# Where the attention mask of batches 1 and 2 is applied: a multiply on VectorE in place of an accumulating matmul on TensorE

## The chip, the cores and the metric

The kernel runs on one core of one Trainium2 chip. The metric is the device time of one execution in microseconds (us); the kernel before takes 332.73 us, the median of three runs (332.69 to 332.88). Engines are named as in the profile: PE is the matrix engine (PEld is its weight load), DVE the vector engine, ACT the scalar engine with the exponential, POOL the engine that issues most of the loads, SP the one that issues the stores and the DMA transposes.

## The reference

Sparse attention over 8 batches, 8 heads, 576 positions and 64 values per head, followed by a feed-forward block on the 4608 tokens:

```python
scores = scale * np.matmul(q, k.transpose(0, 1, 3, 2))
rel = pos[:, None] - pos[None, :]
mask_local = (rel >= 0) & (rel < 32)                                    # heads 0 to 3
mask_strided = (rel >= 0) & (pos[None, :] % 32 == pos[:, None] % 32)    # heads 4 to 7
scores = np.where(masks[None], scores, -1000000000.0)
attn = softmax(scores)                                                  # over the last axis
x = (attn @ v)    # rearranged to [4608 tokens, 512]
h = x @ w_in                                                            # 512 -> 2048
r = np.maximum(h, 0.0)
out = (s * (r * r) + b) @ w_out                                         # 2048 -> 512
```

## The kernel before

Only the tiles of the score matrix that the mask lets through are computed. Heads are taken in pairs: a batch has two local pairs (m = 0, 1) of 6 tiles each, 128 keys by 2 x 96 queries, and two strided pairs (m = 2, 3) of 8 tiles each, 72 keys by 2 x 72 queries. A group of tiles (2 local or 3 strided) shares a PSUM bank and one exponential. The mask is applied in one of two ways, chosen by the batch number `b`. Line numbers of the profile that matter here: 426 is the mask matmul, 429 the score matmul, 443 the exponential, 451 the multiply by the mask.

```python
    TB, SB, AB, F1B, F2B = 1, 2, 1, 2, 2
    PE_MASK = 3
    ps = {tag: [psum.tile([128, PS], FP32, name=f"ps_{tag}{i}") for i in range(n)]
          for tag, n in (("t", TB), ("s", SB), ("a", AB), ("f1", F1B), ("f2", F2B))}
    # ...
        per_s = 2 if loc else 3

        def score(i, group):
            g, n = i // per_s, min(per_s, nt - i // per_s * per_s)

            def f():
                # ...
                if b < PE_MASK:
                    nc.tensor.matmul(                                    # L426
                        out=st["s", g][0:nk, c:c + 2 * nq], lhsT=ident[0:nk, 0:nk],
                        rhs=neg_loc if loc else neg_str, start=True, stop=False)
                nc.tensor.matmul(                                        # L429
                    out=st["s", g][0:nk, c:c + 2 * nq], lhsT=(...),      # k of the tile
                    rhs=st["q"][:, i].rearrange("d e c -> d (e c)"), start=b >= PE_MASK, stop=True)

            s = Step(f, (2 if b < PE_MASK else 1) * (2 * nq / 2.4 + 8), needs=[("q", id_), ("k", id_)],
                     group=group if i % per_s == 0 else None)
            # ...
                def ex(eng):
                    pt = ptp.tile([128, 2 * per_s, nq], FP16, tag="pt" + sfx,
                                  bufs=7 if loc else 6, name="pt")
                    nc.scalar.activation(                                # L443
                        out=pt[0:nk, 0:2 * n].rearrange("k t c -> k (t c)"),
                        in_=st["s", g][0:nk, 0:2 * n * nq], func=AF.Exp, scale=scale)

                def ms(eng):
                    mask = (mask_loc if loc else mask_str)[:, None, :].to_broadcast([nk, 2 * n, nq])
                    nc.vector.tensor_tensor(                             # L451
                        out=pt[0:nk, 0:2 * n], in0=pt[0:nk, 0:2 * n], in1=mask, op=ALU.mult)

                s.posts = [([key], {"A": 170 + 0.83 * 2 * n * nq}, ex, [("e", id_, g), group]),
                           ([("e", id_, g)], {"V": 150 + 0.52 * 2 * n * nq}, ms, [("p", id_, g)])]
                if b < PE_MASK:
                    s.posts = [([key], {"A": 170 + 0.83 * 2 * n * nq}, ex, [("p", id_, g), group])]
```

`neg_loc` and `neg_str` hold 0 where the mask lets through and -30000 elsewhere; the identity times that tile, accumulated under the scores, makes the exponential 0 there. `mask_loc` and `mask_str` hold 1 and 0. The tiles `pt` are then weights for the product with v (line 481); its column of ones gives the sum of each row, so that the division (reciprocal 496, multiply 507) needs no reduction. The normalized x is transposed (529, or by DMA for the local pairs from batch 2 on) into `xT`, of which the feed-forward block reads 512 tokens at a time (a block, `T`; 9 in all):

- 574: first projection, 64 matmuls of 512 columns for a block; ACT or DVE applies the relu (592, 594), DVE squares (598, into `gT`).
- 609: second projection, again 64 matmuls; DVE scales and adds the bias (620) and the result is stored. For block 0, 16 matmuls more (632) make the bias term.

The order of all this is fixed when the program is built. A planner keeps a clock (`plan.t`), in which a step on PE has the length given to `Step`, and every piece of follow-up work has a cost for each engine that may do it; it takes the engine that would end first, and the next PE step whose inputs are ready on this clock:

```python
    def step_ready(self, s):
        r = self.ready_at(s.needs)
        # ... and the PSUM group's bank must be released
    # ...
        if cand is not None and (att_done < due() or main is None):
            s = att[cand][at_i[cand]]        # a step of attention
            plan.emit(s)
        elif main == 1:
            plan.emit(f1[i1])                # first projection
        elif main == 2:
            plan.emit(f2[i2])                # second projection
        elif i1 >= 16 or not keep_running(plan.next_time()):
            plan.advance()                   # nothing is ready: the plan's clock moves on
```

Semaphores keep the data right whatever the real times are; the plan only decides the order in each engine's stream. Loads of q and k of batch b + 2 are issued once batch b's transposes are planned and v of batch b + 1 is fetched, and loads of v of batch b + 2 once batch b's products with v are planned.

Of the kernel before, what the change touches and what calls it, by code (L numbers as in the profile page):

```python
# [110 lines left out]
def kernel(  # L111
# [202 lines left out]


    TB, SB, AB, F1B, F2B = 1, 2, 1, 2, 2
    PE_MASK = 3
    ps = {tag: [psum.tile([128, PS], FP32, name=f"ps_{tag}{i}") for i in range(n)]
          for tag, n in (("t", TB), ("s", SB), ("a", AB), ("f1", F1B), ("f2", F2B))}

# [18 lines left out]
    def pair_steps(b, m):  # L339
# [76 lines left out]
        def score(i, group):  # L416
# [3 lines left out]
            def f():  # L420
                if i % per_s == 0:
                    st["s", g] = bank(group)
                c = i % per_s * 2 * nq
                if b < PE_MASK:

# [4 lines left out]
                    out=st["s", g][0:nk, c:c + 2 * nq], lhsT=(st["k"][:, i * nq:i * nq + nk] if loc else st["k"][:, i, 0:SQ]),  # L430
# [4 lines that stand above are left out]
            if i % per_s == n - 1:  # L435
# [11 lines left out]
                def ms(eng):  # L447
# [8 lines left out]
                            [("p", id_, g)])]  # L456
                if b < PE_MASK:
                    s.posts = [([key], {"A": 170 + 0.83 * 2 * n * nq}, ex, [("p", id_, g), group])]
# [445 lines left out]
```

The softmax here doesn't subtract the row's maximum and nothing guards it: scores larger than these inputs give would overflow.

## Time and profile before

| | before |
|---|---|
| time, median of 3 runs | 332.73 us |
| span of the profiled execution | 330.6 us |
| PE busy, matmuls | 322.2 us (97%), 2480 |
| DVE busy | 193.4 us (58%), 529 instructions |
| ACT busy | 170.4 us (52%), 321 |
| POOL busy | 85.6 us (26%), 123 |
| mask matmuls (line 426) | 36 of 192 columns, 48 of 144; first and last start 9.7 and 80.3 us |
| multiplies by the mask (line 451) | 60, 20.0 us in all; first and last start 87.6 and 198.2 us |

The page gives busy times per engine, the span in 40 slices of 8.3 us (each digit a tenth of busy time), the chain of work that ended last, and groups of instructions by line. A matmul's duration in it is its latency; matmuls overlap, and the step from one to the next is read from the view in order of time. Attention work ends at about 200 us on PE's stream and the rest of the span is feed-forward alone.

### The profile page before, as it was taken

What the parts mean: (1) busy time and instruction counts of PE and PEld (TensorE: products, weight loads), DVE (VectorE), ACT (ScalarE), POOL (GpSimd) and SP (SyncE); (2) the same over time, 40 slices, a digit from 0 to 9 for tenths busy, and PEclk for the clock granted to TensorE, in tenths of its full rate; (3) what the DMA queues carried; (4) which work ended last, traced back from release to release, by engine and by line L of the source; (5) the groups of instructions that cost most, each with busy time, mean ns of one, the idle gap of its engine ahead of it and who ended that gap; (6) DMA issues with size and microseconds to landing.
All of it is one profiled execution on the core that took longest, in us unless ns stands there. A gap on an engine that the chain in (4) does not pass through costs nothing.

```text
span 330.6 us, 6484 instructions
## 1 busy us (share of the span) xinstructions
PE 322.2 (97%) x2480; PEld 185.0 (56%) x2480; DVE 193.4 (58%) x529; ACT 170.4 (52%) x321; POOL 85.6 (26%) x123
## 2 busy tenths in 40 slices
PE   8998999999999999999999999999999999999995
PEld 3764755567666566566665665544544544444442
DVE  6657638587886877778778866633333333333311
ACT  3766833388788576587576753331432433243100
POOL 6481657810944624724710000000000000000000
PEclk9999999999999999999999999999999999999999
DMA  8999999996797996995995003010001100101021
GB/s 118 183 165 204 215 170 164 220 174 70 116 137 99 165 94 132 169 107 101 187 110 91 32 15 87 20 47 32 32 32 43 54 32 35 63 3 62 32 95 63
DMA packets 73176, 32.80 MB, mean 99 GB/s; under 512 B 54586, under 2 KB 67514, under 8 KB 73146
## 3 DMA queue, kind: packets, MB, share of 16 engines
q0 software_dynamic: 50032, 18.65, 57.8%
q1 hardware_dynamic: 23114, 13.74, 18.1%
q8 instruction: 19, 0.31, 0.4%
q14 instruction: 11, 0.09, 0.1%
HBM read 38.15 MB, written 9.44 MB: 144 GB/s over the span
## 4 chain that ended last, share of the span: by engine, by line
PE 87%; DMA 7%; POOL 2%; ACT 2%; issue 1%; DVE 0%; SPq 0%; POOLq 0%; ACTq 0%
PE ps_f L609 37%; PE ps_f L574 35%; DMA ql<-in_q_dram 5%; PE ps_s L429 4%; PE ps_a L481 4%; PE ps_t L357 3%; DMA w_out_sb<-in_v_dram 2%; PE ps_t L529 1%; PE ps_s L426 1%; PE ps_a L632 1%; ACT qD_loc L286 1%; POOL w_in L273 1%; POOL v_loc L286 1%; PE ps_f L481 0%; ACT kT_loc L286 0%
## 5 line engine op out<-in xcount | busy, mean ns | idle before, releaser
L609 PE MATMUL ps_f<-w_out_sb,gT 128*128 128x512 f16 x576 | 148.7, 379 | 0.0
L592 ACT ACTIVATE u<-ps_f 128x512 f16<-128x512 f32 x136 | 80.7, 597 | 87.5 <-PE ps_f L574 72.9
L574 PE MATMUL ps_f<-xT,w_in_sb 128*128 128x512 f16 x432 | 116.0, 379 | 0.8 <-DMA w_in_sb<-in_moe_w_in_dram 0.8
L598 DVE TENSOR_TENSOR gT<-u 128x512 f16<-128x512 f16 x144 | 59.4, 418 | 62.6 <-ACT u L592 62.0
L609 PEld LDWEIGHTS <-gT 128*128 128x128 f16 x576 | 54.2, 98 | 54.0
L574 PEld LDWEIGHTS <-w_in_sb 128*128 128x128 f16 x432 | 46.1, 113 | 34.8 <-DMA w_in_sb<-in_moe_w_in_dram 1.2
L443 ACT ACTIVATE pt<-ps_s 128x384 f16<-128x384 f32 (+2 forms) x96 | 43.7, 488 | 16.0 <-PE ps_s L429 14.8
L620 DVE SCALAR_TENSOR_TENSOR o<-ps_f,s_sb,bcs 128x512 f32<-128x512 f32 x36 | 26.8, 745 | 22.9 <-PE ps_f L609 22.9
L507 DVE TENSOR_TENSOR x_nat<-ps_a,rec 72x256 f16<-72x256 f32 (+1 forms) x76 | 34.9, 460 | 1.2
L481 PEld LDWEIGHTS <-pt 72*72 72x72 f16 (+1 forms) x448 | 29.3, 120 | 10.8
L574 PE MATMUL ps_f<-xT,w_in 128*128 128x512 f16 x136 | 35.2, 379 | 0.1
L260 POOL DMA_DIRECT2D v_loc<-in_v_dram x28 | 24.1, 871 | 2.0 <-DMA ql<-in_q_dram 0.7
L496 DVE RECIPROCAL rec<-ps_a 72x4 f32<-72x4 f32 (+1 forms) x76 | 13.7, 180 | 17.2 <-PE ps_a L481 16.4
L574 PEld LDWEIGHTS <-w_in 128*128 128x128 f16 x144 | 15.3, 114 | 11.0
L265 POOL DMA_DIRECT2D v_str<-in_v_dram x16 | 13.8, 865 | 16.2 <-PE ps_a L481 6.8
L429 PE MATMUL ps_s<-qD_str,kTs 128*72 128x144 f16 x128 | 16.3, 226 | 0.2 <-ACT kTs L286 0.2
L429 PE MATMUL ps_s<-qD_loc,kT_loc 128*128 128x192 f16 x96 | 16.1, 246 | 0.3 <-ACT kT_loc L286 0.2
L481 PE MATMUL ps_a<-v_str,pt 72*72 72x65 f16 x204 | 15.5, 197 | 0.0
L429 PEld LDWEIGHTS <-kTs 128*72 128x72 f16 x128 | 12.0, 114 | 4.0 <-ACT kTs L286 0.4
L286 ACT COPY qD_loc<-ps_t 64x576 f16<-64x576 f16 x16 | 10.1, 633 | 3.7 <-PE ps_t L357 3.6
L529 PEld LDWEIGHTS <-x_nat 72*128 72x128 f16 (+1 forms) x152 | 8.8, 98 | 5.4 <-DVE x_nat L507 1.2
L664 POOL COPY gate<-kTs 1x1 f16<-1x1 f16 x8 | 2.0, 251 | 37.6 <-DMA kTs<-ks 37.6
(92 smaller groups left out, 295.7 us busy)
## 6 DMA issues: line engine op xcount, KB each, us to landing
out_dram<-o SPq DMA_DIRECT2D x36, 256.0 KB, 2.0
ql<-in_q_dram POOLq DMA_DIRECT2D x8, 288.0 KB, 5.1
kl<-in_k_dram POOLq DMA_DIRECT2D x8, 288.0 KB, 6.3
v_loc<-in_v_dram POOLq DMA_DIRECT2D x28, 80.0 KB, 9.1
w_out_sb<-in_moe_w_out_dram POOLq DMA_DIRECT2D x4, 512.0 KB, 11.8
qs<-in_q_dram POOLq DMA_DIRECT2D x6, 288.0 KB, 8.0
ks<-in_k_dram POOLq DMA_DIRECT2D x6, 288.0 KB, 8.6
v_str<-in_v_dram POOLq DMA_DIRECT2D x16, 72.0 KB, 6.9
```

Of the source, the lines that this page charges most:

```text
L260: nc.gpsimd.dma_start(out=vl[:, h, 1:LT, 0:D], in_=rest[:, h])
L265: nc.gpsimd.dma_start(out=vs[:, h, :, 0:D], in_=v[b, 4 + h].rearrange("(p j) d -> p j d", j=ST))
L286: {"A": nc.scalar.copy, "V": nc.vector.tensor_copy, "P": nc.gpsimd.tensor_copy}[eng](**kw)
L429: nc.tensor.matmul(out=st["s", g][0:nk, c:c + 2 * nq], lhsT=(st["k"][:, i * nq:i * nq + nk] if loc else st["k"][:, i, 0:SQ]), rhs=st["q"][ ...
L443: nc.scalar.activation(out=pt[0:nk, 0:2 * n].rearrange("k t c -> k (t c)"), in_=st["s", g][0:nk, 0:2 * n * nq], func=AF.Exp, scale=scale)
L481: nc.tensor.matmul(out=st["a"][0:nq, j % per, :], lhsT=st["pt", g][0:nk, i, :], rhs=vt[0:nk, 2 * mm + e, j, :])
L507: nc.vector.tensor_tensor(out=st["x"][:, j0:j0 + per, 64 * e:64 * e + 64], in0=st["pa", e, j][0:nq, 0:per, 0:D], in1=st["rec", e, j][0:nq, ...
L574: nc.tensor.matmul(out=gts["h", T, ft], lhsT=(w_in_sb[min(ft // 4, 2) - 1][:, ct, :] if ft > 3 else w_in0[ct]).rearrange("p (c x l) -> p c ...
L592: nc.scalar.activation(out=gts["u", T, ft], in_=gts["h", T, ft], func=AF.Relu)
L598: nc.vector.tensor_tensor(out=gts[T][:, ft, :], in0=u, in1=u, op=ALU.mult)
L609: nc.tensor.matmul(out=gts["o", T, ts], lhsT=gts[T][:, ft, ts * 128:(ts + 1) * 128], rhs=w_out_sb[:, ft, :], start=(ft == 0), stop=(ft == ...
L620: nc.vector.scalar_tensor_tensor(out=o, in0=gts["o", T, ts], scalar=s_sb[:, 0:1], in1=bcs, op0=ALU.mult, op1=ALU.add)
```

## The change

The constant `PE_MASK` goes from 3 to 1. It is the number of batches whose mask is added by a matmul. With 3, batches 0, 1 and 2 use the matmul, and batches 3 to 7 the multiply on DVE; with 1, batch 0 alone uses the matmul. It is for taking matmuls from the engine with the most work and giving DVE the masking of batches 1 and 2.

The words that came with the change ("First quarter of w_in in four transfers; k transposed by DMA from batch 4 on and ahead of the next loads; work on later transfers placed later, in place of: First quarter of w_in in four transfers") tell of other things, which both kernels contain. The whole difference between the two programs' texts is this:

```diff
-    PE_MASK = 3
+    PE_MASK = 1
```

The constant is read in four places, all of them shown above: whether the mask matmul is issued, whether the score matmul starts the accumulation, the length of the step on the plan's clock, and whether a multiply on DVE is posted.

## The prediction

> **What bounds the kernel now.** I read the page from the top (busy shares, slices), then the chain of work that ended last, then the matrix engine's (PE's) waits, and last the stretch from 35 to 90 us as a table by stage and in order of time, because only there does batch 1 or 2 run.
>
> ```profile
> PE 322.2 (97%) x2480; PEld 185.0 (56%) x2480; DVE 193.4 (58%) x529; ACT 170.4 (52%) x321; POOL 85.6 (26%) x123
> PE   8998999999999999999999999999999999999995
> DVE  6657638587886877778778866633333333333311
> PE 87%; DMA 7%; POOL 2%; ACT 2%; issue 1%; DVE 0%; SPq 0%; POOLq 0%; ACTq 0%
> ```
>
> The reader is to see that PE is busy nearly everywhere and is 87% of the chain that sets the end; VectorE (DVE) never appears in that chain, though it is 60 to 90% busy up to slice 27. "Busy" alone would not prove a bound, since matmuls overlap. The waits do. Nine are listed for PE in the whole span, the longest 1.1 us at the very start; these are three of them, and none lies between 67 and 90 us:
>
> ```profile
> PE ps_f L574 <- DMA w_in_sb<-in_moe_w_in_dram: 0.8, 1, 0.8
> PE ps_t L529 <- ACT kT_loc L286: 0.3, 1, 0.3
> PE ps_s L429 <- ACT kT_loc L286: 0.2, 1, 0.2
> ```
>
> So after about 35 us, PE waits for almost nothing: its instruction stream is the clock. The table by stage shows what the other engines do meanwhile (columns: stretch, length, busy us and instructions of PE, PEld, DVE, ACT, POOL, then clock, DMA share, GB/s):
>
> ```profile
> 38.00:44.00 6.00, 6.00 (x65) 4.60 (x63) 2.40 (x5) 4.65 (x11) 1.94 (x3) 1.00 1.10 204
> 44.00:50.00 6.00, 6.00 (x29) 2.74 (x28) 1.14 (x3) 0.60 (x1) 4.05 (x5) 1.00 1.81 160
> 61.00:66.40 5.40, 4.99 (x57) 3.13 (x56) 2.42 (x8) 2.37 (x5) 3.99 (x5) 1.00 1.23 249
> 66.40:72.00 5.60, 5.60 (x62) 3.97 (x59) 5.16 (x15) 4.97 (x12) 1.58 (x2) 1.00 1.83 188
> ```
>
> DVE has ample room from 38 to 50 us (3.5 busy of 12) and is crowded from 66.4 to 72 (5.16 of 5.60). The cost of a mask matmul is not its 227 or 246 ns, which is latency, but the step from one start to the next:
>
> ```profile
> 38.30 0.24 PE L429 MATMUL ps_s<-qD_loc,kT_loc 128*128 128x192 f16 x1
> 38.38 0.24 PE L426 MATMUL ps_s<-neg_loc,ident 128*128 128x192 f16 x1
> 38.46 0.25 PE L429 MATMUL ps_s<-qD_loc,kT_loc 128*128 128x192 f16 x1
> 74.87 0.23 PE L426 MATMUL ps_s<-neg_str,ident 72*72 72x144 f16 x1
> 74.94 0.23 PE L429 MATMUL ps_s<-qD_str,kTs 128*72 128x144 f16 x1
> 75.00 0.23 PE L426 MATMUL ps_s<-neg_str,ident 72*72 72x144 f16 x1
> 123.18 0.54 PE L429 MATMUL ps_s<-qD_str,kTs 128*72 128x144 f16 x6
> ```
>
> Start to start is 80 to 85 ns for a local mask (I use 83) and 60 to 70 ns for a strided one (65). The last line is a later batch, without mask matmuls: six scores in 0.54 us, so (0.54 - 0.226) / 5 = 63 ns each. Scores don't become slower when their masks go; each mask removed gives its whole step back.
>
> **What the Trainium skill says.** "TensorE: Matmul & The Clock Gate", section "Back-to-back issue gap", gives N/2.4 + 2.5 ns for a warm isolated gap: 82.5 ns at 192 columns and 62.5 at 144. The trace agrees (83 and 65). The same section gives 131 ns sustained at 512 columns; this trace has 216 (1.08 us for five in the chain in order of time), and I use the trace's. "VectorE: DVE Perf Modes", section "The perf-mode tier table", puts a 16-bit `tensor_tensor` in SBUF at the doubled rate; the mask multiply at 384 elements takes 348 ns against 549 for the multiply of the same size that reads PSUM, which fits. "SBUF — State Buffer", section "Who interferes with whom", says that a DVE operation with two SBUF inputs contends with GpSimd instructions that read SBUF, and infers that descriptor generation isn't hit. The trace agrees as far as it goes: the 15 multiplies from 140 to 170 us, while POOL issues loads, take 4.90 us together, and the 15 from 170 to 200 us, with POOL idle, 4.94. So I charge nothing for contention.
>
> **The change part by part.** The words given with the change name transfers and a transpose by DMA; the diff alters one constant, and both kernels hold those things. What remains: batches 1 and 2 lose the matmul that adds the mask before the exponential and gain a DVE multiply after it, as batches 3 to 7 already have.
>
> *Removed from PE.* Per batch 2 local pairs of heads x 6 tiles and 2 strided pairs x 8. For two batches 24 local and 32 strided: 24 x 0.083 + 32 x 0.065 = 1.99 + 2.08 = 4.1 us, half in each batch.
>
> *Added to DVE.* One multiply per score group. Per batch 6 local groups of 384 elements, 4 strided of 432 and 2 of 288. For two batches 12 x 0.348 + 8 x 0.364 + 4 x 0.295 = 8.3 us (means from the groups by shape). DVE would go from 193.4 to about 201.7 us busy.
>
> *Moved.* The order of every engine's stream is fixed ahead by a planner inside the kernel, which simulates the run with its own costs. The shorter score steps and new posts shift its clock after batch 1's first score (35 us), so later interleaving is redrawn, and some copies go from DVE to ACT. Nothing before 35 us should move.
>
> *Batch 2 (65 to 81 us), on the path.* PE has the first projection of token block 1 to fill with, and DVE's delay only makes batch 2's results later. Those are first needed for block 2: block 1 still has 128 matmuls x 0.216 = 27.6 us from 66.5 us on, besides attention work. DVE takes 4.1 us more where 65 to 81 us holds 12.7 busy of 16, and ACT 12.8; that spills, but the whole stretch from 89 to 200 us runs with multiplies on DVE at 75 to 83% and PE busy in all but 0.14 us. So I count batch 2's saving in full: 2.0 us.
>
> *Batch 1 (35 to 43 us), only partly on the path.* Its multiplies are hidden: exponentials end by 44 us and the first product with v runs at 50.3 us, when v has arrived. But its PE time was filler too. From 44 to 64.7 us, PE fills with the second projection of block 0 (64 matmuls and 16 for the bias), and at its end it needs batch 1's last x transposed: the ACT copy to xT ends at 66.16, and block 1 starts at 66.46. If v's landing and the chain product, reciprocal, multiply, transpose, copy keep their times, 2 us saved at 40 us return as a hole before 66 us. Against that, DVE waits 1.5 us there for the product at 62.93, while PE works through second-projection matmuls that the planner put ahead; with less filler that chain tightens. I count 60%: 1.2 us.
>
> *Sum.* 2.0 + 1.2 = 3.2 us, less 0.5 us for the redrawn order (PE now idles little from 67 to 231 us, so redrawing can hardly improve it): 2.7 us saved, 332.7 - 2.7 = 330.0 us.
>
> **The rivals.** *Everything is returned (4.1 us).* For: PE is 87% of the chain. Against: the tight end of batch 1. It would give 328.6 us. *DVE becomes the bound in batch 2.* For: 5.16 of 5.60 us busy from 66.4 to 72. If 2 to 4 us of holes appear, the time is 331 to 333. Against: there is a block of filler, ACT can take copies, and the later batches run so. *The hole before block 1 takes all of batch 1's saving and the longer latency more:* 330.7 to 332. For: the 0.35 us wait at 65.06 shows that the edge is already reached. *An unlucky order* delays a fetch of a later batch (fetches wait for earlier steps of the plan) and opens a hole of several us: 334 to 338. Against: v and q/k are fetched about one block ahead; in the profile, PE waits for none of these loads after 35 us.
>
> **Range and chances.** The gain is limited by 4.1 us, 1.2% of the time, so "faster by over 2%" needs something the diff doesn't contain. Low end: full gain and a little luck in the order, 328.3. High end: batch 1's saving lost and 2 us of new holes, 332.9. Slower by over 2% needs about 7 us of holes, only by the last rival: 3%.
>
> **What would show each step.** Mask matmuls from 84 to 28 and none after about 17 us; DVE multiplies by a mask from 60 to 84; DVE busy near 201 us. Batch 2: no new PE wait on DVE from 67 to 100 us. Batch 1: the first projection of block 1 starts at 65 to 66 us, instead of 66.46, with about 1 us of PE idle from 50 to 66. From 231 us on, the same stream, 2 to 4 us earlier. I am wrong if PE waits for a masked tile or for `gT` for over 1 us in total, if a fetch of a later batch shows up among PE's waits, or if block 1 starts no earlier than before.

## The result, and the profile after

The changed kernel takes 329.91 us (median of six, 328.95 to 330.71), the kernel before 332.70 (six, 332.63 to 332.88): ratio 0.9912, 95% interval 0.9895 to 0.9929. Measured again on another chip, it took 329.53 us against 332.67, ratio 0.9893 (0.9873 to 0.9912). It is faster, by about 1%.

The page of the changed kernel, busy shares, slices and chain:

```profile
PE 318.7 (97%) x2424; PEld 181.7 (55%) x2424; DVE 201.2 (61%) x552; ACT 171.6 (52%) x322; POOL 84.8 (26%) x123
PE   8898899999999999999999999999999999999995
DVE  5566946698877768676878777586442423332311
PE 85%; DMA 7%; ACT 4%; POOL 2%; issue 1%; DVE 0%; SPq 0%; POOLq 0%
```

PE lost exactly the 56 mask matmuls. DVE gained 7.8 busy us and is still absent from the chain; ACT went from 2% of it to 4%. One thing shows that nobody asked for: DVE's busy stretch reaches two or three slices further to the right. Mask matmuls and multiplies, by line:

```profile
L426 PE MATMUL ps_s<-neg_str,ident x16: 223/226/233, 14.5 to 18.6; 72*72 72x144 f16 x16
L426 PE MATMUL ps_s<-neg_loc,ident x12: 242/246/249, 10.4 to 13.5; 128*128 128x192 f16 x12
L451 DVE TENSOR_TENSOR pt<-pt,mask_loc x42: 320/357/361, 38.5 to 212.5; 128x384 f16<-128x384 f16 x42
L451 DVE TENSOR_TENSOR pt<-pt,mask_str x42: 293/370/380, 41.6 to 224.5; 72x432 f16<-72x432 f16 x28, 72x288 f16<-72x288 f16 x14
```

The last multiply starts at 224.5 us, against 198.2 before. The same stretches as before, and PE's waits for other engines that matter:

```profile
38.00:44.00 6.00, 5.65 (x56) 3.82 (x55) 5.83 (x17) 5.36 (x13) 2.12 (x3) 1.00 1.07 210
44.00:50.00 6.00, 6.00 (x31) 2.75 (x29) 1.26 (x4) 0.97 (x3) 3.71 (x5) 1.00 1.83 146
61.00:66.40 5.40, 5.16 (x61) 3.23 (x59) 2.87 (x9) 4.20 (x9) 4.53 (x5) 1.00 1.23 225
66.40:72.00 5.60, 5.60 (x57) 3.65 (x57) 4.91 (x17) 5.44 (x11) 2.85 (x4) 1.00 1.63 192
```

```profile
PE ps_f L574 <- DMA w_in_sb<-in_moe_w_in_dram: 1.3, 1, 1.3
PE ps_t L357 <- POOL kp L286: 0.9, 1, 0.9
PE ps_s L429 <- ACT pt L443: 0.3, 1, 0.3
PE ps_f L609 <- DVE gT L598: 0.3, 1, 0.3
PE ps_t L357 <- ACT xT L286: 0.2, 1, 0.2
```

From 38 to 44 us, DVE goes from 2.40 to 5.83 busy of 6; 3.0 us of that are batch 1's multiplies. PE has three small new waits: for the exponential at 39 us, for xT at 65 and for gT at 90. The waits for w_in and kp lie before 32 us, and POOL's instruction order is that of before; they are loads that landed later in this execution.

**A measure without the loads.** Because landing times of the first loads move all that follows, I compare stretches that begin at batch 1's first score: from there to the first matmul of block 1 (T = 1), and from there to the last matmul's start. All are read from the profiled executions. Times of different rows can come from different chips; each ratio below is taken against the kernel before on the same chip (332.42 to 332.70 us).

| run | first score of batch 1, us | to block 1, us | from block 1 to the last matmul, us | sum | time, us (median) |
|---|---|---|---|---|---|
| before | 35.46 | 31.00 | 259.96 | 290.96 | 332.70 |
| changed | 36.67 | 29.30 | 258.46 | 287.75 | 329.91 |
| changed, again | 35.43 | 29.47 | 258.47 | 287.94 | 329.53 |
| b2_only | 35.47 | 31.00 | 259.14 | 290.14 | 331.70 |
| b1_only | 35.04 | 29.48 | 258.92 | 288.40 | 330.19 |
| pace_only | 35.24 | 31.01 | 259.69 | 290.70 | 332.38 |
| no_mul_b12 | 35.88 | 29.29 | 258.36 | 287.65 | 329.59 |
| order_kept | 34.96 | 29.73 | 259.03 | 288.76 | 330.55 |
| mask_old_pace | 36.19 | 29.48 | 258.68 | 288.16 | 329.67 |
| mask_all_pe | 39.58 | 31.00 | 269.88 | 300.88 | 342.61 |
| k_dma_b2 | 35.47 | 29.30 | 257.93 | 287.23 | 328.85 |
| slow_pace | 34.96 | 29.42 | 257.77 | 287.19 | 329.27 |
| k_dma_and_pace | 35.67 | 29.30 | 257.43 | 286.73 | 329.18 |
| none_pe | 39.95 | 32.07 | 259.00 | 291.07 | 337.03 |

The sums separate what the times blur: 3.0 to 3.2 us saved, 1.5 to 1.7 of it before block 1 and 1.5 after. The two stretches are not quite the two batches: in the kernel before, four of batch 2's mask matmuls (0.33 us) lie ahead of block 1. The stretch behind the last matmul's start is outside the sum; it takes 4.2 us in most profiles and 4.5 to 4.7 in five (b2_only, mask_old_pace, k_dma_b2, k_dma_and_pace, none_pe). The row of none_pe holds 3.4 us at half the clock (see there).

**Where 4.1 us became 3.** A stall here is a matmul's step to the next start minus the median step of its shape in the kernel before; shorter steps count against it. Summed from batch 1's first score on, stalls are 1.7 us before, 2.4 in the changed kernel and 2.6 in it again. The stretch holds 55 of the 56 mask steps (batch 1's first lies just ahead of it), 4.0 us; less 0.8 to 1.0 us of added stalls, they make the 3.2 to 3.0 us measured. The two largest stalls, in order of time on PE:

```profile
38.40 0.66 PE L429 MATMUL ps_s<-qD_loc,kT_loc 128*128 128x192 f16 x4
38.90 0.42 PE L357 MATMUL ps_t<-ident,ks 72*128 72x72 f16 x8
39.66 0.33 PE L429 MATMUL ps_s<-qD_loc,kT_loc 128*128 128x192 f16 x2 [0.34 <-ACT pt L443]
89.91 0.39 PE L609 MATMUL ps_f<-w_out_sb,gT 128*128 128x512 f16 x1
90.58 0.39 PE L609 MATMUL ps_f<-w_out_sb,gT 128*128 128x512 f16 x1 [0.28 <-DVE gT L598]
```

Eight transposes of 32 ns from 38.90 end at 39.16, and the next score starts at 39.66: 0.5 us in which both score banks wait for an exponential. Scores without mask steps come at twice the rate, and ACT doesn't. At 89.91 the step to the next matmul is 0.67 us instead of 0.216.

### The profile page after: what moved, and what is told of

Read it like the earlier page. It is cut to its first block, busy times and chain, and to the rows that moved or that the text cites. A ratio compares the mean times of both kernels' runs of the same rounds, so it can differ in the third digit from the quotient of the medians.

```text
span 328.6 us, 6386 instructions
## 1 busy us (share of the span) xinstructions
PE 318.7 (97%) x2424; PEld 181.7 (55%) x2424; DVE 201.2 (61%) x552; ACT 171.6 (52%) x322; POOL 84.8 (26%) x123
## 4 chain that ended last, share of the span: by engine, by line
PE 85%; DMA 7%; ACT 4%; POOL 2%; issue 1%; DVE 0%; SPq 0%; POOLq 0%
PE ps_f L609 37%; PE ps_f L574 34%; DMA ql<-in_q_dram 5%; PE ps_s L429 4%; PE ps_a L481 4%; PE ps_t L357 3%; DMA w_out_sb<-in_v_dram 2%; PE ps_t L529 1%; PE ps_a L632 1%; ACT pt L443 1%; ACT qD_str L286 1%; ACT qD_loc L286 1%; POOL w_in L273 1%; POOL v_loc L286 1%; ACT xT L286 0%
## 5 line engine op out<-in xcount | busy, mean ns | idle before, releaser
L609 PE MATMUL ps_f<-w_out_sb,gT 128*128 128x512 f16 x576 | 151.6, 379 | 0.3 <-DVE gT L598 0.3
L574 PE MATMUL ps_f<-xT,w_in_sb 128*128 128x512 f16 x432 | 118.3, 379 | 1.3 <-DMA w_in_sb<-in_moe_w_in_dram 1.3
L443 ACT ACTIVATE pt<-ps_s 128x384 f16<-128x384 f32 (+2 forms) x96 | 44.6, 488 | 17.0 <-PE ps_s L429 16.2
L481 PEld LDWEIGHTS <-pt 72*72 72x72 f16 (+1 forms) x448 | 36.9, 119 | 13.9 <-DVE pt L451 0.2
L481 PE MATMUL ps_a<-v_str,pt 72*72 72x65 f16 x204 | 22.8, 196 | 0.0
L429 PE MATMUL ps_s<-qD_str,kTs 128*72 128x144 f16 x128 | 18.8, 226 | 0.2 <-ACT kTs L286 0.2
L429 PE MATMUL ps_s<-qD_loc,kT_loc 128*128 128x192 f16 x96 | 17.3, 246 | 0.7 <-ACT pt L443 0.3
L481 PE MATMUL ps_a<-v_loc,pt 128*96 128x65 f16 x150 | 17.1, 203 | 0.0
L451 DVE TENSOR_TENSOR pt<-pt,mask_loc 128x384 f16<-128x384 f16 x42 | 14.4, 351 | 3.9 <-ACT pt L443 3.6
L451 DVE TENSOR_TENSOR pt<-pt,mask_str 72x432 f16<-72x432 f16 (+1 forms) x42 | 14.1, 348 | 3.6 <-ACT pt L443 3.3
```

The source lines that it names most:

```text
L429: nc.tensor.matmul(out=st["s", g][0:nk, c:c + 2 * nq], lhsT=(st["k"][:, i * nq:i * nq + nk] if loc else st["k"][:, i, 0:SQ]), rhs=st["q"][ ...
L443: nc.scalar.activation(out=pt[0:nk, 0:2 * n].rearrange("k t c -> k (t c)"), in_=st["s", g][0:nk, 0:2 * n * nq], func=AF.Exp, scale=scale)
L451: nc.vector.tensor_tensor(out=pt[0:nk, 0:2 * n], in0=pt[0:nk, 0:2 * n], in1=mask, op=ALU.mult)
L481: nc.tensor.matmul(out=st["a"][0:nq, j % per, :], lhsT=st["pt", g][0:nk, i, :], rhs=vt[0:nk, 2 * mm + e, j, :])
L574: nc.tensor.matmul(out=gts["h", T, ft], lhsT=(w_in_sb[min(ft // 4, 2) - 1][:, ct, :] if ft > 3 else w_in0[ct]).rearrange("p (c x l) -> p c ...
L609: nc.tensor.matmul(out=gts["o", T, ts], lhsT=gts[T][:, ft, ts * 128:(ts + 1) * 128], rhs=w_out_sb[:, ft, :], start=(ft == 0), stop=(ft == ...
```

## The experiments

The theory (A): PE's stream is the clock, so each mask matmul removed returns its step. Rivals: (B) a side effect, the pace of attention. The plan gives attention its place by `due()`, which is scaled by the length of batch 1's steps; without mask steps that length is 2144 ns less (12 x 88 + 16 x 68 ns on the plan's clock), so attention of the later batches is spread further. (C) DVE crowded in batch 2. (D) the hole before block 1 takes batch 1's share.

**after_again**: the changed kernel, unaltered.

> The changed kernel again, for its spread (six times lay between 328.95 and 330.71 us, those of before within 0.25 us). If the spread comes from when the first loads land, a profile with a time near 329 us shows batch 0's first score before 10 us (10.8 us in the profile at 330.71) and everything after it earlier by the same amount. If it comes from later, the first score stands at 10.8 us again and the difference appears after 60 us.

329.53 us (328.94 to 329.90). The two profiled spans differ by 1.07 us (328.6 and 327.6), and batch 1's first score by 1.24 us (36.67 and 35.43); from there on they agree within 0.2. Its batch 0's first score stands at 10.4 us, only 0.4 earlier, so the rest of the shift comes between 10 and 36 us. The wait for w_in is the piece that differs: its step is 1.67 us in one and 0.73 in the other. So in these two profiles the spread is the landing of early loads; neither of the two expected pictures came as it was drawn.

**b2_only**, **b1_only**: one batch at a time. The edits:

```diff
-    PE_MASK = 3          # b2_only
+    PE_MASK = 2
```

```diff
-    PE_MASK = 3          # b1_only; the tests become "b in PE_MASK"
+    PE_MASK = (0, 2)
```

> Only batch 2 goes over to the multiply; batch 1 keeps its mask matmuls, and so the pace of attention, which is derived from batch 1's length, stays that of before. Theory A (PE's stream is the clock): 28 mask matmuls go from a stretch with filler, 2.0 us less, 330.7 us. Theory B (the new pace, which stretched attention from 212 to 231 us, made the gain): no gain, 332.5 to 333 us. Theory C (DVE crowded from 66 to 82 us): 331.5 us or more, with PE waits on a masked tile or on gT.

> Only batch 1 goes over to the multiply; batch 2 keeps its mask matmuls; the pace is that of the changed kernel. Theory A: 60% of batch 1's 2.0 us, 331.5 us, block 1's first projection 0.5 to 1.2 us earlier than 66.46 us. Theory B: the whole gain, about 330 us. Rival D (the hole before block 1 takes all): block 1 starts at 66.5 us and the time is 332.5 us or, with the pace's share, whatever the run of the pace alone gives.

b2_only takes 331.70 us, ratio 0.9971 (0.9955 to 0.9987): 1.0 us saved, 0.8 in the sum. b1_only takes 330.19 us, ratio 0.9914 (0.9895 to 0.9933): 2.5 us saved, 2.6 in the sum. Theory A had this the wrong way round in size: batch 1 was to give 1.2 and batch 2 2.0. Batch 1 alone gives even more than its mask steps (2.6 against 2.0 us), and 1.0 of it comes after block 1, where its matmuls no longer are: its stalls are 1.1 us, 0.6 fewer than before. The largest one of before, 0.51 us at the wait for kT_loc ahead of block 1, is gone in the redrawn order, and the steps of products with v after block 1's start, spread further, average 34 ns instead of 38. Rival D falls: block 1 came 1.5 us nearer to batch 1's first score. For b2_only, PE's waits after the start show rival C in small:

```profile
PE ps_a L481 <- DVE pt L451: 0.5, 1, 0.5
PE ps_t L357 <- ACT xT L286: 0.4, 1, 0.4
PE ps_t L529 <- ACT kT_loc L286: 0.3, 1, 0.3
PE ps_f L609 <- DVE gT L598: 0.2, 1, 0.2
```

A product with v waits 0.5 us for a tile that DVE multiplies by the mask. The stalls of this run add up to 1.2 us more than before, against 2.0 us of mask steps removed. In the changed kernel, whose order is another, that wait isn't there.

**pace_only**, **mask_old_pace**: the pace alone, and the masks without it.

```diff
-    batch_ns = sum(s.ns for p in att[4:8] for s in p)
+    batch_ns = sum(s.ns for p in att[4:8] for s in p) - 2144.0   # pace_only, in the kernel before
+    batch_ns = sum(s.ns for p in att[4:8] for s in p) + 2144.0   # mask_old_pace, in the changed kernel
```

> The kernel before, all masks where they were, but the batch length from which the pace of attention is derived is smaller by 2144 ns, as the change makes it (batch 1 without mask steps). Theory A: PE's work is the same and it was never idle after 67 us, so the time is 332.7 us within 0.4. Theory B: about 330 us, the whole gain without a mask moved. A third outcome, in between, gives the pace's share.

> The changed kernel with the old pace of attention (batch length raised by 2144 ns). Theory A, with the pace worth nothing on its own (0.3 us in the run of the pace alone): 329.7 us within 0.7. If the pace helps through the products with v, whose steps were 1 us shorter in all where attention was spread furthest, 330.5 us and attention ends near 212 us. A crowded DVE from 89 to 130 us would give 331 us.

pace_only: 332.38 us, ratio 0.9991 (0.9975 to 1.0007), no difference that the times show, 0.3 us in the sum. mask_old_pace: 329.67 us, ratio 0.9916 (0.9901 to 0.9931), as the changed kernel; 0.2 to 0.4 us more in the sum. Rival B falls as the cause: the pace moved the end of attention (last product with v at 211 us before, not at about 200, where the scores end; 231 changed, 220 with the old pace, 249 with the pace alone) and almost nothing else.

**no_mul_b12**: the multiplies of batches 1 and 2 left out of the changed kernel, whose order on PE stays as it is. The two batches are then unmasked.

```diff
-                    nc.vector.tensor_tensor(
+                    b in (1, 2) or nc.vector.tensor_tensor(
```

> The changed kernel with the 24 multiplies of batches 1 and 2 left out and everything else in the changed kernel's order (these two batches are then not masked). If the multiplies are hidden behind PE, as the prediction said, the time is that of the changed kernel within 0.4 us (329.1 to 330.1) and PE's stall of 0.46 us on gT at 89 us stays. If DVE's extra 8.3 us costs anything, it shows here: up to 1.2 us less (328.5), with the stalls at 84 to 91 us gone.

329.59 us, ratio 0.9911 (0.9897 to 0.9925): the same as with the multiplies, and every engine has the same instructions in the same order but for these 24. They are hidden. Its stall on gT is still there, so the multiplies of batches 1 and 2 don't make it; what does is not shown (in order of time on PE):

```profile
88.99 0.39 PE L609 MATMUL ps_f<-w_out_sb,gT 128*128 128x512 f16 x1
89.66 0.39 PE L609 MATMUL ps_f<-w_out_sb,gT 128*128 128x512 f16 x1 [0.28 <-DVE gT L598]
```

**order_kept**: the mask matmuls of batches 1 and 2 left out of the kernel before, no multiply put in, the plan's costs as before, so that every engine keeps its old order. These batches are unmasked.

```diff
-                if b < PE_MASK:      # around the mask matmul alone
+                if b < 1:
-                    rhs=..., start=b >= PE_MASK, stop=True)
+                    rhs=..., start=b >= 1, stop=True)
```

> The kernel before, with the mask matmuls of batches 1 and 2 left out and nothing put in their place (these batches are then not masked), in the order of the kernel before. PE's stream shrinks by 4.1 us. If the redrawn order cost the 1.1 us between 4.1 and the 3.0 us measured, this gives 328.6 us. If the rest was lost to waits for the exponential in batch 1 and to the hole before block 1, which no order avoids, it gives 329.3 to 330 us and these stalls are in its stream too.

330.55 us, ratio 0.9938 (0.9922 to 0.9954), 2.2 us in the sum: less than the changed kernel saves, though it has less work. Its waits on PE after the start:

```profile
PE ps_t L357 <- ACT xT L286: 0.4, 1, 0.4
PE ps_t L529 <- ACT kT_loc L286: 0.3, 1, 0.3
PE ps_a L481 <- DVE x_nat L507: 0.2, 1, 0.2
PE ps_f L357 <- ACT qD_str L286: 0.2, 1, 0.2
```

Two of the four, xT and kT_loc, stand at 62 to 64.5 us, at the edge before block 1: the old order, kept while PE is faster, runs into the latencies there. Against no_mul_b12, which also has neither mask matmuls nor multiplies in these batches but the new order, it is 1.1 us longer in the sum, which is the difference of the stalls, 3.45 us here and 2.34 there. Both halves of what was expected of it fail: the redrawn order isn't what costs, it is what saves 1.1 us (a difference of the new interleaving with its pace, of which the pace is 0.2 to 0.4).

What the order does before block 1 can be read from the second projection's matmuls (line 609) on both sides of batch 1's first product with v. Each pair of lines goes from batch 1's first score to that product, and from there to block 1, in the kernel before, the changed kernel and order_kept (columns: stretch, length, busy us and number of matmuls, of weight loads, then clock, DMA share, GB/s; a matmul that only ends in the stretch is counted too, so go by the weight loads):

```profile
35.46:50.30 14.84, 4.21 (x18) 1.76 (x18) 1.00 1.39 189
50.30:66.45 16.15, 11.83 (x47) 3.97 (x46) 1.00 1.47 192
36.67:51.35 14.68, 5.51 (x24) 2.35 (x24) 1.00 1.40 182
51.35:65.96 14.61, 11.00 (x41) 3.46 (x40) 1.00 1.38 193
34.96:48.53 13.57, 4.21 (x18) 1.76 (x18) 1.00 1.39 192
48.53:64.69 16.16, 11.84 (x47) 3.98 (x46) 1.00 1.37 195
```

In the old order the product comes 1.3 us sooner and the stretch behind it keeps its 16.16 us. The new order puts six second-projection matmuls where the masks were, ahead of the product, and the stretch behind it, with 40 of them in place of 46, shrinks to 14.61 us (14.79 in the second profile). The 0.7 us by which the new order is better after block 1 are not taken apart.

**mask_all_pe**: the opposite dose.

```diff
-    PE_MASK = 3
+    PE_MASK = 8
```

> The opposite dose: all eight batches use the mask matmul. Five batches more, 60 local and 80 strided mask matmuls: 60 x 0.083 + 80 x 0.065 = 10.2 us. Theory A: 332.7 + 10.2 = 342.9 us, within 1, since PE has filler all the time there and DVE's relief is worth nothing. If DVE or ACT bound anything between 89 and 200 us, relieving DVE of 20 us gives some of it back: 339 to 341 us.

342.61 us, ratio 1.0307 (1.0289 to 1.0325): 10.1 us more than its neighbour before (332.49), 9.9 in the sum, where the steps gave 10.2 and stalls are 0.3 us fewer. (The profile is of an execution of 346.60 us: PE waited 2.9 us for w_in and had half the clock from 32.5 to 35.9 us. The sum begins after both.) DVE fell to 178.9 busy us and it returned nothing:

```profile
PE 333.7 (97%) x2620; PEld 196.0 (57%) x2620; DVE 178.9 (52%) x471; ACT 171.4 (50%) x319; POOL 84.9 (25%) x123
```

**none_pe**: the dose beyond the change, batch 0 as well.

```diff
-    PE_MASK = 1
+    PE_MASK = 0
```

> All batches use the multiply, batch 0 too: 28 mask matmuls less from 10 to 19 us, 2.0 us by their steps. If only filler time counts (batch 0 runs before there is any work to fill with, and its end waits for the loads of w_in and of batch 1's q, which land at about 29 and 31 us), nothing comes of it: 329.7 us within 0.7. If PE's stream were the clock there too, 327.7 us. If the longer chain of batch 0 (multiply after the exponential) delays block 0, 330.5 us or more.

337.03 us, ratio 1.0119 (1.0088 to 1.0150): 4.5 us slower than before and 7 slower than the changed kernel. Of the three expectations, only the third, 330.5 us or more, holds; it names the direction, but not the wait and the clock that the trace shows. In order of time:

```profile
12.86 0.70 SPq L708 DMA_DIRECT2D mask_loc<-mask_loc  x1
17.05 1.06 DVE L451 TENSOR_TENSOR pt<-pt,mask_loc 128x384 f16<-128x384 f16 x2 [5.17 <-DMA mask_loc<-mask_loc]
18.15 0.46 DVE L286 COPY kTs<-ps_a 128x576 f16<-128x576 f16 x1
19.02 0.38 PE L429 MATMUL ps_s<-qD_str,kTs 128*72 128x144 f16 x3 [4.33 <-DVE kTs L286]
```

The mask tile is loaded late: its load is issued at 12.86 us and lands at 17.0, and in the changed kernel the first multiply starts only at 38.5 us. Here DVE's first multiply waits 5.17 us for it, the copy of k, whose input PE had written by 13.0, stands behind the multiply in DVE's stream, and PE waits 4.33 us for the copy. That is half of the delay: block 0's first matmul starts at 27.2 us instead of 18.9. The other half falls in a stretch with half the clock (columns: stretch, length, PE busy and matmuls, granted clock, DMA share, GB/s):

```profile
15.00:19.00 4.00, 0.00 (x0) 1.00 0.88 120
19.30:26.10 6.80, 6.36 (x73) 0.50 1.08 170
39.80:43.20 3.40, 3.25 (x23) 0.50 1.05 212
```

PE runs no matmul from 15 to 19 us, and from 19.3 us on, and again from 39.8, it is granted half the clock; a matmul of 512 columns then steps at 427 ns instead of 216. The mean clock is 0.985 to 0.990 in all six executions of this kernel and 0.993 or more in those of all other kernels. The two stretches last 10.2 us; work that is twice as fast at the full clock would fill 5.1 us, so by this estimate the clock costs up to 5 us and may be as large a part of the loss as the wait. How much an earlier load of the mask tiles would give back is open: that variant wasn't run.

**k_dma_b2**, **slow_pace**, **k_dma_and_pace**: does anything beat the changed kernel?

```diff
-        k_by_dma, x_by_dma = b >= 3, b >= 2
+        k_by_dma, x_by_dma = b >= 2, b >= 2                                     # k_dma_b2
-    batch_ns = sum(s.ns for p in att[4:8] for s in p)
+    batch_ns = sum(s.ns for p in att[4:8] for s in p) - 1000.0                   # slow_pace
```

> The changed kernel, with the strided k of batch 2 transposed by DMA as well (batches 3 to 7 have it so). PE loses 16 transposes of 32 ns, 0.5 us, and ACT or DVE two copies of 0.46 to 0.64 us. If PE's stream is the clock: 329.2 us. If the fetch of batch 3, which then waits for that DMA transpose, comes late, or batch 2's strided scores wait for it: 330 to 333 us, with PE waits on a DMA.

> The changed kernel with a batch length smaller by 1000 ns more, so that attention is spread further (it ended at 231 us). If shorter runs of products with v, whose weight loads hide behind 512-column matmuls, are a gain: products with v about 0.5 us less in all and 329.2 us. If the 512-column steps pay it back, as they did in the run of the pace alone: 329.7 us within 0.5.

> The two small steps together: strided k of batch 2 by DMA (328.85 us alone) and attention spread further (329.27 alone), against 329.5 to 329.9 for the changed kernel. If both are shorter PE streams, they add: 328.0 to 328.5 us. If they are within what the redrawn order does by chance, anything from 328.5 to 330.

328.85 us (0.9902, 0.9868 to 0.9937), 329.27 (0.9905, 0.9888 to 0.9922) and 329.18 (0.9900, 0.9883 to 0.9917). In the sums they are shorter than the changed kernel (287.75 and 287.94) by 0.5 to 0.7, 0.6 to 0.8 and 1.0 to 1.2 us, so the small steps do shorten the stream and nearly add. In the times this is not visible: the first loads land at other moments, the stretch behind the last matmul is 4.56 us instead of 4.20 in the two profiles with k by DMA, and the three intervals overlap those of the changed kernel. k_dma_b2 does wait for its DMA transpose on PE, as was feared, but for 0.3 us only. No version is shown to beat it.

## Why the prediction was right, and which step wasn't

The time, 329.91 us, is within 0.1 of the 330.0 predicted. Part of that is luck, as terms of the sum were off in opposite directions; without the loads the saving is 3.0 to 3.2 us, not 2.7.

- *What a mask matmul costs.* Right. 83 and 65 ns from start to start, taken from six lines of the order of time, gave 10.2 us for five batches; the opposite dose measured 10.1.
- *DVE's 8.3 us are hidden.* Right: DVE goes from 193.4 to 201.2 us busy, and with the multiplies left out at the same PE order the time is the same. The rival "DVE becomes the bound in batch 2" is seen only in b2_only, as a wait of 0.5 us.
- *Batch 1: 60%, 1.2 us.* The mechanism was right (less filler, and the chain before block 1 tightens: from 16.15 to 14.61 us behind the first product with v), the size too small: 1.5 to 1.7 us before block 1 in the changed kernel, 1.5 in b1_only. With the order of before it is 1.27, almost what the 60% said, so what was mis-sized is what the plan makes of it. The hole that was to take the rest, "about 1 us of PE idle from 50 to 66", isn't there: PE idles 0.24 us from 50 us to block 1, and 0.41 before. The feared limit, v's landing, did not hold either: in order_kept the first product with v comes 1.3 us nearer to batch 1's first score, without a wait for v.
- *Batch 2 in full, 2.0 us, "less 0.5 us for the redrawn order".* Their sum, 1.5, is what was measured after block 1, by luck. The split was wrong: with the old order kept, only 0.9 us arrives after block 1 (259.96 to 259.03), and with batch 2 alone changed 0.8, so batch 2 isn't returned in full by itself; and the redrawing doesn't cost 0.5 us but brings 1.1 us over both stretches. The argument that "redrawing can hardly improve it" compared with a stream that still had its mask steps. Once they are gone the old order is no longer good, and the plan finds the better one.
- *What was not seen.* The constant also sets the pace of attention, through the length of batch 1's steps. Attention ended 19 us later. The pace is worth 0.3 us in the stream and nothing that the times show, but it was missed: the length of the step was named among the four places that read the constant, and that batch 1's length also scales the pace was not drawn from it. The statement that from 231 us on the stream would be the same, 2 to 4 us earlier, held all the same (2.0 and 3.1 us in the two profiles), because 231 us is just where attention now ends.
- *What would show each step.* Mask matmuls 84 to 28, none after 18.6 us (17 was said); multiplies 60 to 84; block 1 at 65.97 us here and at 64.90 in the second profile (65 to 66 was said); no fetch among PE's waits after 35 us; PE's stall on gT 0.46 us, under the 1 us that would have spoken against it. One sign failed: from 67 to 100 us there was to be no new PE wait on DVE, and the one on gT at 90 us is new, though the multiplies of batches 1 and 2 don't make it.
- *A reading.* DVE is not 60 to 90% busy up to slice 27 in the kernel before: slices 3, 6 and 8 read 5, 3 and 5, and the last 6 is slice 26. Nothing in the sum rests on it.

## What to carry to other kernels

Where one engine is busy without waits, price a removed instruction at its step to the next start and not at its duration. What comes back of that price depends on the small waits of the new order (here for an exponential, a transposed tile, a squared tile): 3.0 to 3.2 of 4.1 us with both batches, 0.8 of 2.0 with batch 2 alone, 2.6 of 2.0 with batch 1 alone, 9.9 of 10.2 in the opposite dose. When the order of instructions is computed from costs, test the edit with the order kept as well as with it redrawn; here the redrawing was a third of the gain. And before moving work to another engine at the start of a kernel, look up when its operands land and read the granted clock: with a mask tile that landed at 17.0 us and half the clock after the wait for it, the same change for one batch more cost 7 us instead of saving 2.

## What the runs showed of the hardware that I had not expected

A product with v of a local pair (96 columns of weights, 65 moving) takes 45 ns from start to start within a run of such products, and 29 ns when it is the first after another kind of matmul (medians). In the kernel before, products with v come in runs of 6 (local pairs) and 4 (strided), in the changed one, spread further, mostly in ones and twos (75 runs against 162 of both kinds after block 1's start). One line of the kernel before and one of the changed kernel, each with the line after it:

```profile
119.99 0.43 PE L481 MATMUL ps_a<-v_loc,pt 128*96 128x65 f16 x6
120.25 0.38 PE L574 MATMUL ps_f<-xT,w_in_sb 128*128 128x512 f16 x1
```

```profile
128.32 0.19 PE L481 MATMUL ps_a<-v_loc,pt 128*96 128x65 f16 x1
128.35 0.39 PE L574 MATMUL ps_f<-xT,w_in_sb 128*128 128x512 f16 x1
```

Six take 0.26 us, 43 ns each; the single one 0.03. No run isolates why. The gain is mostly paid back: after block 1's start, the steps of products with v add up to 12.02 us in the second profile of the changed kernel (334 products) instead of 12.65 (336), and those of the first projection's 512 matmuls to 111.20 instead of 110.76.

The landing of the first loads varied by about 1 us between executions of one program (step at the wait for w_in: 0.73 us in one profile of the changed kernel, 1.67 in the other). The kernel before, which lay within 0.25 us in its first six executions, ranged from 331.88 to 335.20 us in 33 on another chip; none of those was profiled, so the cause of that range is not shown.

PE's granted clock fell to half for 3.4 or 6.8 us at a time, in two kernels only: none_pe at 19.3 and 39.8 us, mask_all_pe at 32.5 us, each time within 1.2 us of the end of a wait on PE (4.33, 1.35 and 2.93 us). In every other profile it was full from about 7 us to the last matmul. What sets the half clock off is not shown.
